# A decayed-state attention and a soft mixture of experts in one kernel: a pipeline of 24 chunk steps over eight heads, rewritten as 32 units of a head pair times three chunks

## The chip, the cores and the metric

The kernel runs on one core of a Trainium2 chip. The metric is the device time of one execution in microseconds (us); three executions of the kernel before took 251.03, 251.22 and 251.81 us, so its time is 251.22 us. A core has a matrix engine (TensorE, in the profile PE, its weight loads PEld), a vector engine (VectorE, DVE), a scalar engine (ScalarE, ACT) and GpSimd (POOL). SyncE (SP) here only issues transfers. Sixteen DMA engines carry the transfers of all queues. Matrix products are written to PSUM; the other data lie in SBUF.

## The reference

`r`, `k` and `v` are float32 arrays of shape 4 x 8 x 768 x 48 (batch, head, time, width), `w` and `u` are 8 x 48. The first half is a recurrence over time for every batch and head. Its output, with the heads laid side by side, is the 3072 x 384 input of the second half, a soft mixture of 8 experts with 4 slots each.

```python
# first half, for every batch b and head h
state = 0                                   # 48 x 48
for t in range(768):
    y[t]  = r[t] @ (state + outer(u * k[t], v[t]))
    state = w[:, None] * state + outer(k[t], v[t])

# second half: x is 3072 x 384, phi 384 x 32, w1 8 x 384 x 1024, w2 8 x 1024 x 384
logits = x @ phi
d = softmax over the 3072 rows of logits    # dispatch weights
slot_input = d.T @ x                        # 32 x 384: 8 experts x 4 slots
slot_out[e] = relu(slot_input[e] @ w1[e]) @ w2[e]
c = softmax over the 32 slots of logits     # combine weights
out = c @ slot_out                          # 3072 x 384
```

The maxima that the softmaxes subtract are left out here and in both kernels.

A chunked form of the recurrence lets the matrix engine do the work: inside a chunk of 128 time steps, with k and r scaled by powers of w, the part that stays in the chunk is a masked product of the scaled r and k with v, and the part from earlier chunks is the scaled r times a carried 48 x 48 state. The term with `u` is a number per time step and head, times v.

## The kernel before

A step is one chunk of one batch, with all eight heads: 4 x 6 = 24 steps. The transfers of a step are r, k and v of 128 x 8 x 48 floats; every row of 48 floats (192 bytes) lies by itself in the source. A weight of one expert is loaded by GpSimd's queue in some of the steps and turned from float32 to bfloat16 on the way.

```python
for b in range(B):
    state = st_pool.tile([D, H, D], bf, name="state")
    nc.vector.memset(state[:], 0.0)
    for c in range(nC):
        n_tile = b * nC + c
        issue_w_dma(n_tile - 8)                # w1[e] for 8 steps, then w2[e] for 8 steps
        r_ld, k_ld, v_ld = ...                 # in_pool, 3 buffers each
        nc.sync.dma_start(out=r_ld[:], in_=r[b, :, t0:t0 + C, :].rearrange("h p d -> p h d"))
        nc.sync.dma_start(out=k_ld[:], in_=k[b, :, t0:t0 + C, :].rearrange("h p d -> p h d"))
        nc.scalar.dma_start(out=v_ld[:], in_=v[b, :, t0:t0 + C, :].rearrange("h p d -> p h d"))
        nc.scalar.copy(v_bf[:], v_ld[:])
        nc.gpsimd.tensor_mul(rr2_cd[:], r_ld[:], W_neg3)      # scaled r
        nc.gpsimd.tensor_mul(kk_cd[:], k_ld[:], W_k3)         # scaled k
        nc.gpsimd.tensor_mul(ku[:], k_ld[:], u_rep3)
        nc.gpsimd.tensor_mul(ku[:], ku[:], r_ld[:])
        nc.vector.tensor_reduce(d_diag[:], ku[:], axis=mybir.AxisListType.X, op=ALU.add)
        for h in range(H):
            nc.tensor.transpose(rr2_dp[:, h, :], rr2_cd[:, h, :], ident[:])
            nc.tensor.transpose(kk_dp[:, h, :], kk_cd[:, h, :], ident[:])
        nc.scalar.copy(rr2_dc[:], rr2_dp[:])
        nc.scalar.copy(kk_dc[:], kk_dp[:])
        for h in range(H):
            nc.tensor.matmul(AT_p[:, h, :], kk_dc[:, h, :], rr2_dc[:, h, :])
        nc.vector.tensor_mul(AT_s[:], AT_p[:], mask_ut[:, None, :].to_broadcast([128, H, 128]))
        for h in range(H):
            nc.tensor.matmul(y_p[:, h, :], AT_s[:, h, :], v_bf[:, h, :], start=True, stop=False)
            nc.tensor.matmul(y_p[:, h, :], rr2_dc[:, h, :], state[:, h, :], start=False, stop=True)
        nc.gpsimd.tensor_mul(dv[:], v_bf[:], d_diag[:, :, None].to_broadcast([128, H, D]))
        nc.vector.tensor_add(x_sbuf[:, n_tile, :]..., y_p[:], dv[:])
        for h in range(H):
            nc.tensor.matmul(s_p[:, h, :], kk_cd[:, h, :], v_bf[:, h, :])
        nc.vector.tensor_add(state2[:], state[:], s_p[:])
        nc.gpsimd.tensor_mul(state[:], state2[:], w128_dc[:, :, None].to_broadcast([D, H, D]))
```

After all steps come three stages, one after the other: the routing (for each of 24 row tiles: three transposes of x, three products with phi, an exponential, the column sums, three products for the slot inputs, one transpose of the exponentials), the experts (`ht_p`, a rectifier for every 128 x 4 result, `so_p`), and the output:

```python
for ni in range(nN):                            # 24 tiles
    nc.tensor.matmul(o_p[:], LexpT[:, ni, :], so_sm[:, :])
    nc.vector.tensor_scalar_mul(o_s[:], o_p[:], rsum_r[:, ni:ni + 1])
    nc.sync.dma_start(out=out_ap[:, ni, :], in_=o_s[:])       # o_s has 3 buffers
```

Of the kernel before, what the change touches and what calls it, by code (L numbers as in the profile page):

```python
# [10 lines left out]
def kernel(  # L12
# [12 lines left out]
    nc = tc.nc  # L25
    B, H, S, D = r.shape
# [3 lines left out]
    assert Nn == B * S and Dm == H * D  # L30
# [3 lines left out]
    Spe = ES // E  # L34
    nN = Nn // C
    nM = Dm // C

    f32 = mybir.dt.float32
    bf = mybir.dt.bfloat16
    AF = mybir.ActivationFunctionType  # L40
    ALU = mybir.AluOpType

    cst = ctx.enter_context(tc.tile_pool(name="cst", bufs=1))

    ident = cst.tile([128, 128], bf)
    make_identity(nc, ident)

    mask_ut = cst.tile([128, 128], f32)
    make_upper_triangular(nc, mask_ut, val=1.0, diag=False)

    w_rep = cst.tile([128, H * D], f32, name="w_rep")
    nc.sync.dma_start(out=w_rep[:], in_=w.flatten().partition_broadcast(128))
    u_rep = cst.tile([128, H * D], f32, name="u_rep")
    nc.sync.dma_start(out=u_rep[:], in_=u.flatten().partition_broadcast(128))

    logw = cst.tile([128, H * D], f32, name="logw")
    nc.scalar.activation(out=logw[:], in_=w_rep[:], func=AF.Ln)

    iotash = cst.tile([128, 1], mybir.dt.int32, name="iotash")
    nc.gpsimd.iota(iotash, pattern=[[0, 1]], base=-C, channel_multiplier=1)  # L60
    ishf = cst.tile([128, 1], f32, name="ishf")
    nc.vector.tensor_copy(ishf[:], iotash[:])
    ishf2 = cst.tile([128, 1], f32, name="ishf2")
    nc.vector.tensor_scalar(out=ishf2[:], in0=ishf[:], scalar1=-1.0, scalar2=-1.0,
                            op0=ALU.mult, op1=ALU.add)

    W_neg = cst.tile([128, H * D], f32, name="W_neg")
    nc.scalar.activation(out=W_neg[:], in_=logw[:], func=AF.Exp, scale=ishf[:])  # L68
    W_k = cst.tile([128, H * D], f32, name="W_k")
    nc.scalar.activation(out=W_k[:], in_=logw[:], func=AF.Exp, scale=ishf2[:])  # L70

    w_hd = cst.tile([H, D], f32, name="w_hd")
    nc.sync.dma_start(out=w_hd[:], in_=w)
    ident_f32 = cst.tile([H, H], f32, name="ident_f32")
    make_identity(nc, ident_f32)
    w128_dc = cst.tile([D, H], f32, name="w128_dc")
    with tc.tile_pool(name="wT_ps", bufs=1, space=bass.MemoryType.PSUM) as wT_ps:
        wT_p = wT_ps.tile([D, H], f32, name="wT_p")
        nc.tensor.transpose(wT_p[:], w_hd[:], ident_f32[:])
        nc.scalar.activation(out=w128_dc[:], in_=wT_p[:], func=AF.Ln)  # L80
    nc.scalar.activation(out=w128_dc[:], in_=w128_dc[:], func=AF.Exp, scale=float(C))

    ones_col = cst.tile([128, 1], bf, name="ones_col")
    nc.vector.memset(ones_col[:], 1.0)

    x_pool = ctx.enter_context(tc.tile_pool(name="x_pool", bufs=1))
    x_sbuf = x_pool.tile([128, nN, Dm], bf, name="x_sbuf")
    nF = F // 128
    w1_all = x_pool.tile([128, E, nM, F], bf, name="w1_all")
    w2_all = x_pool.tile([128, E, nF, Dm], bf, name="w2_all")  # L90
    w1_ap = moe_w1.rearrange("e (mo p) f -> p e mo f", p=128)
    w2_ap = moe_w2.rearrange("e (fo p) d -> p e fo d", p=128)

    def issue_w_dma(idx):
        if 0 <= idx < E:
            nc.gpsimd.dma_start(out=w1_all[:, idx, :, :], in_=w1_ap[:, idx, :, :])
        elif E <= idx < 2 * E:
            ee = idx - E
            nc.gpsimd.dma_start(out=w2_all[:, ee, :, :], in_=w2_ap[:, ee, :, :])

    W_neg3 = W_neg[:].rearrange("p (h d) -> p h d", h=H)
    W_k3 = W_k[:].rearrange("p (h d) -> p h d", h=H)
    u_rep3 = u_rep[:].rearrange("p (h d) -> p h d", h=H)

    with tc.tile_pool(name="in_pool", bufs=3) as in_pool, \
         tc.tile_pool(name="st_pool", bufs=2) as st_pool, \
         tc.tile_pool(name="wk_pool", bufs=2) as wk_pool, \
         tc.tile_pool(name="ps_pool", bufs=1, space=bass.MemoryType.PSUM) as ps_pool, \
         tc.tile_pool(name="ps2_pool", bufs=1, space=bass.MemoryType.PSUM) as ps2_pool:

        for b in range(B):
            state = st_pool.tile([D, H, D], bf, name="state")
            nc.vector.memset(state[:], 0.0)

            for c in range(nC):
                n_tile = b * nC + c
                issue_w_dma(n_tile - 8)
                t0 = c * C
                r_ld = in_pool.tile([128, H, D], f32, name="r_ld")
                k_ld = in_pool.tile([128, H, D], f32, name="k_ld")  # L120
                v_ld = in_pool.tile([128, H, D], f32, name="v_ld")
                nc.sync.dma_start(out=r_ld[:], in_=r[b, :, t0:t0 + C, :].rearrange("h p d -> p h d"))
                nc.sync.dma_start(out=k_ld[:], in_=k[b, :, t0:t0 + C, :].rearrange("h p d -> p h d"))
                nc.scalar.dma_start(out=v_ld[:], in_=v[b, :, t0:t0 + C, :].rearrange("h p d -> p h d"))
                v_bf = in_pool.tile([128, H, D], bf, name="v_bf")
                nc.scalar.copy(v_bf[:], v_ld[:])  # L126

                rr2_cd = wk_pool.tile([128, H, D], bf, name="rr2_cd")
                kk_cd = wk_pool.tile([128, H, D], bf, name="kk_cd")
                nc.gpsimd.tensor_mul(rr2_cd[:], r_ld[:], W_neg3)  # L130
                nc.gpsimd.tensor_mul(kk_cd[:], k_ld[:], W_k3)  # L131

                ku = wk_pool.tile([128, H, D], f32, name="ku")
                nc.gpsimd.tensor_mul(ku[:], k_ld[:], u_rep3)  # L134
                nc.gpsimd.tensor_mul(ku[:], ku[:], r_ld[:])  # L135
                d_diag = wk_pool.tile([128, H], f32, name="d_diag")
                nc.vector.tensor_reduce(d_diag[:], ku[:], axis=mybir.AxisListType.X, op=ALU.add)  # L137

                rr2_dp = ps_pool.tile([D, H, C], bf, name="rr2_dp")
                kk_dp = ps_pool.tile([D, H, C], bf, name="kk_dp")  # L140
                for h in range(H):
                    nc.tensor.transpose(rr2_dp[:, h, :], rr2_cd[:, h, :], ident[:])  # L142
                    nc.tensor.transpose(kk_dp[:, h, :], kk_cd[:, h, :], ident[:])  # L143
                rr2_dc = wk_pool.tile([D, H, C], bf, name="rr2_dc")
                kk_dc = wk_pool.tile([D, H, C], bf, name="kk_dc")
                nc.scalar.copy(rr2_dc[:], rr2_dp[:])  # L146
                nc.scalar.copy(kk_dc[:], kk_dp[:])  # L147

                AT_p = ps2_pool.tile([128, H, 128], f32, name="AT_p")
                for h in range(H):  # L150
                    nc.tensor.matmul(AT_p[:, h, :], kk_dc[:, h, :], rr2_dc[:, h, :])  # L151
                AT_s = wk_pool.tile([128, H, 128], bf, name="AT_s")
                nc.vector.tensor_mul(  # L153
                    AT_s[:],
                    AT_p[:],
                    mask_ut[:, None, :].to_broadcast([128, H, 128]),
                )

                y_p = ps_pool.tile([128, H, D], f32, name="y_p")
                for h in range(H):  # L160
                    nc.tensor.matmul(y_p[:, h, :], AT_s[:, h, :], v_bf[:, h, :], start=True, stop=False)  # L161
                    nc.tensor.matmul(y_p[:, h, :], rr2_dc[:, h, :], state[:, h, :], start=False, stop=True)  # L162
                dv = wk_pool.tile([128, H, D], bf, name="dv")
                nc.gpsimd.tensor_mul(dv[:], v_bf[:], d_diag[:, :, None].to_broadcast([128, H, D]))  # L164
                nc.vector.tensor_add(  # L165
                    x_sbuf[:, n_tile, :].rearrange("p (h d) -> p h d", h=H),
                    y_p[:], dv[:])

                s_p = ps_pool.tile([D, H, D], f32, name="s_p")
                for h in range(H):  # L170
                    nc.tensor.matmul(s_p[:, h, :], kk_cd[:, h, :], v_bf[:, h, :])
                state2 = st_pool.tile([D, H, D], f32, name="state2")
                nc.vector.tensor_add(state2[:], state[:], s_p[:])
                nc.gpsimd.tensor_mul(state[:], state2[:], w128_dc[:, :, None].to_broadcast([D, H, D]))  # L174
# [14 lines left out]
    with tc.tile_pool(name="lg_ps", bufs=2, space=bass.MemoryType.PSUM) as lg_ps, \  # L189
# [5 lines left out]
        for ni in range(nN):  # L195
            xt_p = lg_ps.tile([128, nM, 128], bf, name="xt_p")
            for mi in range(nM):
                nc.tensor.transpose(xt_p[:, mi, :], x_sbuf[:, ni, mi * 128:(mi + 1) * 128], ident[:])  # L198
# [95 lines left out]
```

The softmax here doesn't subtract the row's maximum and nothing guards it: scores larger than these inputs give would overflow.

## Time and profile before

The profiled execution spans 249.5 us from its first to its last instruction. The chain that ended last and the busy time in windows divide it:

| stage | from, to (us) | what runs |
|---|---|---|
| start | 0 to 14 | first loads, tables of powers of w |
| 24 chunk steps | 14 to 177.7 | all engines |
| routing | 177.7 to 205.8 | PE 25.0 of 26 us in the middle part |
| experts | 205.8 to 224.3 | 384 matmuls, 64 rectifiers |
| slot outputs turned | 224.3 to 225.7 | 3 transposes |
| output | 225.7 to 249.5 | 24 products, 24 transfers |

Busy times over the span are PE 189.1 us, POOL 144.7, DVE 100.6, ACT 79.2. "Busy" for PE counts each matmul from its start to its end, though they run into each other, so starts of neighbouring matmuls say more than busy time. In a row of a group the last figures before the bar's end are busy us and the mean ns of one; in a window row the columns are PE, PEld, DVE, ACT and POOL busy with counts, the granted clock of the matrix engine, the busy share of the DMA engines and the GB/s that they wrote. That share can pass 1, as packets overlap.

### The profile page before, as it was taken

How to read it: one execution, taken by the hardware profiler on the slowest of the kernel's cores; microseconds unless marked ns; L12 is line 12 of the kernel's file. 1: busy time of each engine (PE TensorE's matmuls, PEld its weight loads, DVE VectorE, ACT ScalarE, POOL GpSimd, SP SyncE). 2: the span in 40 equal slices, each digit the busy share in tenths (PEclk: the TensorE clock that was granted, in tenths of full speed). 3: DMA queues.
4: the chain of work that ended last, by engine and by line, in shares of the span. 5: the costliest groups of instructions: out<-in, count | busy, mean ns of one | idle time of the engine just before them, and what ended most of it. 6: DMA issues, size and time to landing. Idle time of an engine off the chain costs nothing. (4 is left out here: it accounts for less than half of the span.)

```text
span 249.5 us, 4643 instructions
## 1 busy us (share of the span) xinstructions
PE 189.1 (76%) x1828; PEld 137.9 (55%) x1828; DVE 100.6 (40%) x209; ACT 79.2 (32%) x169; POOL 144.7 (58%) x171
## 2 busy tenths in 40 slices
PE   0049898899499999897696579675799978885552
PEld 0047686688277877675475357544566647771110
DVE  1012552653454554344232351434345551116673
ACT  2393433435135235323432133303011115540000
POOL 1389999999999997889578776982100000000000
PEclk9999999999555555555555555555555555555555
DMA  5998699696799999999999989490000000003655
GB/s 120 192 221 161 121 200 201 119 172 137 137 185 133 187 176 177 169 176 167 204 171 189 206 133 124 75 129 0 8 4 1 0 3 3 3 3 119 241 208 189
DMA packets 90581, 32.20 MB, mean 129 GB/s; under 512 B 75968, under 2 KB 87488, under 8 KB 90560
## 3 DMA queue, kind: packets, MB, share of 16 engines
q0 software_dynamic: 11520, 12.58, 32.8%
q1 hardware_dynamic: 54080, 14.60, 25.6%
q10 hardware_dynamic: 24960, 4.72, 10.0%
q8 instruction: 14, 0.23, 0.4%
q14 instruction: 7, 0.06, 0.1%
HBM read 39.77 MB, written 4.72 MB: 178 GB/s over the span
## 5 line engine op out<-in xcount | busy, mean ns | idle before, releaser
L146 ACT COPY rr_dc<-rr_dp 48x1024 bf16<-48x1024 bf16 x24 | 24.1, 1005 | 74.7 <-PE rr_dp L142 63.2
L142 PE MATMUL rr_dp<-ident,rr_cd 128*48 128x128 bf16 x192 | 32.2, 308 | 20.1 <-POOL rr_cd L130 16.1
L161 PE MATMUL y_p<-v_bf,AT_s 128*128 128x48 bf16 x192 | 42.5, 221 | 6.3 <-DVE AT_s L153 6.3
L162 PE MATMUL y_p<-state,rr_dc 48*128 48x48 bf16 x192 | 41.8, 217 | 0.4 <-POOL state L174 0.4
L142 PEld LDWEIGHTS <-rr_cd 128*48 128x48 bf16 x192 | 22.4, 153 | 22.4 <-POOL rr_cd L130 21.2
L153 DVE TENSOR_TENSOR AT_s<-AT_p,mask_ut 128x1024 bf16<-128x1024 f32 x24 | 29.3, 1221 | 12.6 <-PE AT_p L151 12.6
L165 DVE TENSOR_TENSOR x_sbuf<-y_p,dv 128x384 bf16<-128x384 f32 x24 | 13.4, 557 | 51.2 <-PE y_p L162 51.2
L174 POOL TENSOR_TENSOR state<-state,w_dc 48x384 bf16<-48x384 f32 x24 | 19.8, 825 | 22.8 <-PE y_p L162 22.5
L143 PE MATMUL kk_dp<-ident,kk_cd 128*48 128x128 bf16 x192 | 30.5, 308 | 1.2 <-POOL kk_cd L131 1.1
L161 PEld LDWEIGHTS <-AT_s 128*128 128x128 bf16 x192 | 20.0, 104 | 18.7 <-DVE AT_s L153 8.1
L137 DVE TENSOR_REDUCE d_diag<-ku 128x8 f32<-128x384 f32 x24 | 13.2, 548 | 38.7 <-POOL ku L135 38.7
L134 POOL TENSOR_TENSOR ku<-k_ld,u_rep 128x384 f32<-128x384 f32 x24 | 23.7, 987 | 8.1 <-DMA k_ld<-in_k_dram 8.1
L147 ACT COPY kk_dc<-kk_dp 48x1024 bf16<-48x1024 bf16 x24 | 24.1, 1004 | 7.1 <-PE kk_dp L143 7.1
L151 PE MATMUL AT_p<-rr_dc,kk_dc 48*128 48x128 bf16 x192 | 24.3, 303 | 1.6 <-ACT kk_dc L147 1.6
L143 PEld LDWEIGHTS <-kk_cd 128*48 128x48 bf16 x192 | 21.9, 151 | 5.1 <-POOL kk_cd L131 2.6
L162 PEld LDWEIGHTS <-rr_dc 48*128 48x128 bf16 x192 | 19.5, 101 | 9.5
L130 POOL TENSOR_TENSOR rr_cd<-r_ld,W_neg 128x384 bf16<-128x384 f32 x24 | 23.6, 985 | 1.3 <-ACT W_neg L68 1.3
L135 POOL TENSOR_TENSOR ku<-ku,r_ld 128x384 f32<-128x384 f32 x24 | 23.7, 986 | 0.1
L131 POOL TENSOR_TENSOR kk_cd<-k_ld,W_k 128x384 bf16<-128x384 f32 x24 | 23.7, 986 | 0.0
L151 PEld LDWEIGHTS <-kk_dc 48*128 48x128 bf16 x192 | 18.4, 136 | 3.3 <-ACT kk_dc L147 1.8
L164 POOL TENSOR_TENSOR dv<-v_bf,d_diag 128x384 bf16<-128x384 bf16 x24 | 19.7, 823 | 0.4 <-DVE d_diag L137 0.4
L126 ACT CAST v_bf<-v_ld 128x384 bf16<-128x384 f32 x24 | 12.3, 510 | 19.8 <-PE y_p L161 5.6
(63 smaller groups left out, 223.6 us busy)
## 6 DMA issues: line engine op xcount, KB each, us to landing
w_all<-in_moe_w_dram POOLq DMA_DIRECT2D x16, 768.0 KB, 7.8
v_ld<-in_v_dram ACTq DMA_DIRECT2D x24, 192.0 KB, 5.7
r_ld<-in_r_dram SPq DMA_DIRECT2D x24, 192.0 KB, 3.7
k_ld<-in_k_dram SPq DMA_DIRECT2D x24, 192.0 KB, 4.6
out_dram<-o_s SPq DMA_DIRECT2D x24, 192.0 KB, 1.9
w_rep<-in_w_dram SPq DMA_DIRECT2D x1, 192.0 KB, 3.9
u_rep<-in_u_dram SPq DMA_DIRECT2D x1, 192.0 KB, 6.2
phi_f<-in_moe_phi_dram SPq DMA_DIRECT2D x1, 48.0 KB, 1.9
```

The source lines that it names most:

```text
L130: nc.gpsimd.tensor_mul(rr2_cd[:], r_ld[:], W_neg3)
L131: nc.gpsimd.tensor_mul(kk_cd[:], k_ld[:], W_k3)
L134: nc.gpsimd.tensor_mul(ku[:], k_ld[:], u_rep3)
L135: nc.gpsimd.tensor_mul(ku[:], ku[:], r_ld[:])
L142: nc.tensor.transpose(rr2_dp[:, h, :], rr2_cd[:, h, :], ident[:])
L143: nc.tensor.transpose(kk_dp[:, h, :], kk_cd[:, h, :], ident[:])
L146: nc.scalar.copy(rr2_dc[:], rr2_dp[:])
L147: nc.scalar.copy(kk_dc[:], kk_dp[:])
L151: nc.tensor.matmul(AT_p[:, h, :], kk_dc[:, h, :], rr2_dc[:, h, :])
L153: nc.vector.tensor_mul(AT_s[:], AT_p[:], mask_ut[:, None, :].to_broadcast([128, H, 128]),)
L161: nc.tensor.matmul(y_p[:, h, :], AT_s[:, h, :], v_bf[:, h, :], start=True, stop=False)
L162: nc.tensor.matmul(y_p[:, h, :], rr2_dc[:, h, :], state[:, h, :], start=False, stop=True)
```

## The change

The whole kernel is rewritten. A unit is now one pair of heads over three chunks; there are 4 batches x 2 groups of three chunks x 4 pairs = 32 units. The powers of w count over the 384 steps of the three chunks (one frame), so no state has to be rescaled inside a unit: the state before each of its chunks is a prefix sum that PSUM accumulates. The pair's two 48-wide heads lie in a 128-wide tile at 0 and 64, so one transpose serves two heads. All instructions keep the program order on their engine, and each pass of the loop holds stages of up to four units; the routing of finished units lies in the passes too.

What it is for: fewer and larger operations on each engine, GpSimd with two multiplications per unit instead of six per chunk, no stage in which one engine alone works, and an output that is written in larger pieces.

The core of the diff (`O(...)` only records program order; the lines of the old loop, all removed, are those shown above):

```diff
+ def rows(src, b): return src[b].rearrange("h (c p) d -> p (h c) d", p=128)
+ def load_batch(b):                                   # two buffers for each of k, r, v
+     sp.dma_start(out=k_raw[b % 2][:], in_=rows(k, b))
+     sp.dma_start(out=r_raw[b % 2][:], in_=rows(r, b))
+     sp.dma_start(out=v_raw[b % 2][:], in_=rows(v, b))
+ load_batch(0); sp.dma_start(out=phi_f[:], ...); load_batch(1)
+ # w2 by "(p fo) d -> p fo d": eight rows of 384 in one piece for a partition; w1 as before
+ for c in range(L): W_k[:, c, :] and W_r[:, c, :] = Exp(scale * ln w)   # ACT, L = 3
+ def scale(i, j):   pool.tensor_mul(kr[:, j] (two heads at 0 and 64), raw k or r, W_k or W_r)
+ def v_cast(i):     act.copy(vb[:], raw_view(v_raw, i))
+ def t_pe(i):       6 x pe.transpose(Tb[i % 2][:, o:o + C], kr[:, j, c, :], ident[:])
+ def t_evac(i):     act.copy(krT, Tb[i % 2][:, 0:768])
+ def prod_f(i):     dve.tensor_mul(prod, Tb[i % 2][:, 0:384], krT[:, 1])     # k times r, for the u term
+ def a_pe(i):       6 x pe.matmul(Ab[:, e, c*C:(c+1)*C], krT[s, 0, c, :], krT[s, 1, c, :])  # s: 64 rows
+ def mask_f(i):     dve.tensor_mul(AT[:], Ab[:, :, 0:384], mask_ut broadcast)
+ def m_pe(i):       # group 0: 3 matmuls of 288, 192, 96 columns; group 1: ident, Z0 (192), then 192, 96
+     for c in range(nreg): pe.matmul(Mb[:, c*96:nreg*96], kr[:, 0, c, :], v of chunk c repeated, ...)
+     for c in range(L):    pe.matmul(Mb[:, 288+2*c:290+2*c], prod[:, c, :], ucol[:, q, :], ...)
+ def z_evac(i):     dve.tensor_mul(dv, v, Mb u terms); dve.tensor_mul(Z, Mb, bmask)
+                    if g == 0: dve.scalar_tensor_tensor(Z0, Mb, wT, bmask)
+ def y_pe(i):       6 x pe.matmul(48 columns: AT, vb); 2 or 3 x pe.matmul(96 columns: krT, Z)
+                    pe.matmul(Yb[:, 0:288], ident, dv)
+ def y_evac(i):     act.copy(x[:, :, pair], Yb)
+ def route_pe / route_act:   # for each three chunks (four units): 9 transposes of x, 9 products with phi,
+                    # 3 transposes and 12 products of the exponentials; ACT: 3 copies, 1 Exp, 1 copy
+ W_AT = {1: 1, 4: 1, 6: 1, 9: 1, 12: 1, 14: 1, 16: 1, 18: 1, 21: 1, 23: 2, 24: 2, 25: 3}
+ for i in range(-3, nH + nQ + 1):                     # nH = 32, nQ = 4
+     t_pe(i + 2); t_evac(i + 2)
+     scale(i + 3, 0); scale(i + 3, 1); v_cast(i + 3)
+     a_pe(i + 1); mask_f(i + 1)
+     prod_f(i + 2)
+     y_pe(i); y_evac(i)
+     m_pe(i + 1); z_evac(i + 1)
+     route_pe(i); route_act(i)
+     if i == 5: load_batch(2)
+     if i == 13: load_batch(3)
+     W_AT.get(i, 0) x load_w(...)                     # w1[0..7], then w2[0..7]
+ # experts: all 192 matmuls of w1 (columns fo:F:nF), one rectifier per expert on 128 x 32;
+ # then all 192 matmuls of w2, one copy per expert; 3 transposes and one copy
+ # output: row tiles i::24, six PSUM buffers, scaled by DVE and ACT in turn,
+ # transfers of 2, 4, 4, 4, 4, 4, 2 tiles; a partition's rows of one transfer are one piece
- for ni in range(nN): ... (routing, experts and output as stages of their own)
```

## The prediction

> **What bounds the kernel now.** I read the 40 slices first, then the DMA queues, the groups of instructions, the busy time in windows, and last the PE timeline, whose start-to-start times replace its busy time. Slices and queues:
>
> ```profile
> POOL 1389999999999997889578776982100000000000
> PEclk9999999999555555555555555555555555555555
> DMA  5998699696799999999999989490000000003655
> ...
> q0 software_dynamic: 11520, 12.58, 32.8%
> q1 hardware_dynamic: 54080, 14.60, 25.6%
> q10 hardware_dynamic: 24960, 4.72, 10.0%
> ```
>
> GpSimd fills the first 17 slices or so: it has four multiplications of 986 ns and two of about 824 ns per chunk, 5.6 us, and weight issues of about 0.9 us. The chunk steps take (177.7 - 14)/24 = 6.8 us each, so they are GpSimd's pace with some hand-over waits. The waits agree: DVE and ACT wait for PE and POOL, and a wait for a load is rare. But the second bound is near: the DMA row is at 9 from 6 to 143 us. The rest of the span, 71.8 us, is the three late stages (28.1 routing, 19.9 experts with the turned slot outputs, 23.8 output), in which the DMA row is empty or half full and GpSimd idle.
>
> How fast can the loads go? Windows (GB/s is the last column, DMA share before it):
>
> ```profile
> 12.00:14.00 2.00, 0.00 (x0) 0.00 (x0) 0.00 (x0) 1.97 (x4) 0.84 (x1) 1.00 1.32 247
> 15.00:18.00 3.00, 2.19 (x24) 2.06 (x23) 1.10 (x2) 2.97 (x6) 3.00 (x5) 1.00 1.15 213
> 22.00:23.50 1.50, 1.50 (x13) 1.06 (x11) 0.37 (x1) 0.36 (x1) 1.50 (x3) 1.00 1.10 218
> 155.00:158.00 3.00, 1.33 (x14) 1.02 (x14) 2.19 (x4) 0.45 (x1) 2.89 (x4) 0.50 1.30 202
> ```
>
> The first and third are full of 192-byte rows alone (the third from one queue), 218 to 247 GB/s; I take 230. The second is a w1 load, the fourth a w2 load, 202 to 213 GB/s at their bfloat16 destination. So a batch of k, r and v (3.54 MB) needs 15.4 us and a weight (0.786 MB) 3.75 us: all of it 4 x 15.4 + 16 x 3.75 = 122 us of full DMA. In the packets of the trace between 16.5 and 17.5 us, 103 weight packets of 2 KB pass and about 20 of 192 bytes: a weight in flight nearly stops the input rows.
>
> PE, from the timeline (start, length, x count):
>
> ```profile
> 48.99 0.51 PE L171 MATMUL s_p<-v_bf,kk_cd 128*48 128x48 bf16 x8
> ...
> 49.65 1.03 PE L151 MATMUL AT_p<-rr_dc,kk_dc 48*128 48x128 bf16 x8
> ...
> 52.12 0.22 PE L161 MATMUL y_p<-v_bf,AT_s 128*128 128x48 bf16 x1
> 52.27 0.22 PE L162 MATMUL y_p<-state,rr_dc 48*128 48x48 bf16 x1
> 52.42 0.22 PE L161 MATMUL y_p<-v_bf,AT_s 128*128 128x48 bf16 x1
> ```
> ```profile
> 60.66 0.60 PE L151 MATMUL AT_p<-rr_dc,kk_dc 48*128 48x128 bf16 x8
> ```
>
> Eight products of 128 columns in 1.03 us, less the 0.30 us of the last one, over seven: about 105 ns apart, 1.2 columns per ns. The same eight take 0.60 us at 60.66, in the only stretch of fast clock (58.4 to 61.8 us). So the nines of the PEclk row before 58 us are not a fast clock; PE ran at half speed nearly throughout. 48-column products follow 42 ns apart (s_p), but 153 ns apart in y_p, where a 128-row and a 48-row product alternate: about 110 ns for each change of form.
>
> **What the Trainium skill says.** "DMA: Bandwidth & Descriptors", Specifications, asks for at least 512 bytes per transfer for line rate. The trace agrees in direction: 192-byte rows move at 218 to 247 GB/s, the 1536-byte output rows at up to 241 though they come in separate transfers with gaps. The changed kernel keeps the 192-byte rows. Its section "Queues, rings and completion order" says that an engine takes turns between queues by packets, not bytes; that is what starves the 192-byte rows beside 2 KB packets here. "TensorE: Matmul & The Clock Gate", Part 1, gives 107 ns (cold) and 56 ns (warm) for 128 columns; the trace has 105 and, in its one warm stretch, about 60. "TensorEngine Tiling (Array Packing)", Key Properties, says that a change of tiling mode drains the engine; the 153 against 42 ns agree.
>
> **The change, part by part. PE per unit.** Columns: transposes 768; `a_pe` 768; `m_pe` 576 or 480, mean 528, and 6; `y_pe` 6 x 48 + 240 + 288 = 816 (240 is the mean of two and three of 96). Routing per three chunks 9 x 128 + 9 x 32 + 3 x 128 + 12 x 32 = 2208, for a unit 552. Sum 3438 columns, at 1.2 per ns 2.87 us. Two changes of form around the 64-row `a_pe` add 0.2, the tiny products 0.1; if the two 64-row halves overlap, some 0.3 comes off. I take 3.0 us.
>
> **The others per unit.** ACT: 384 elements take 510 ns and 1024 take 1005 (rows L126 and L146), so 213 + 0.773 n: 0.81 (768) + 2 x 0.44 (288) + routing (3 x 0.51 + 0.29 + 0.51)/4 = 0.58, sum 2.3 us. DVE: 384 take 557, 1024 take 1221 (L165, L153), so 158 + 1.04 n: mask 0.96, product 0.36 to 0.56, dv 0.46, Z 0.36, half a Z0 0.13, sum 2.3 to 2.5. GpSimd: two multiplications of 288 at about 0.78, and half a weight issue of 0.9, sum 2.0; eight heads of one chunk are 4/3 units, so 2.7 us against 5.6 plus issues before. No instruction waits for one later than the pass before or the head of its own, so a pass lasts as long as its busiest engine: PE, 3.0 us. Without waits for loads the 32 units take 96 us.
>
> **Loads against units.** First packets came 1.9 us after their issue at 0.75. From 2.65: w_rep 0.7, then k, r, v of batch 0 at 5.1 each: v has landed at about 19.5 with its completion. `v_cast(0)` holds ACT till then; three short filling passes, unit 0 at 22.5. Batch 1 and phi and the weights of passes 1 and 4 end at 2.65 + 0.7 + 30.8 + 0.3 + 7.5 = 42; pass 5 (which casts unit 8) would come at 22.5 + 5 x 3 = 37.5 and waits till 42.5. Batch 2 follows with three weights, 15.4 + 11.2, to 69; pass 13 by the engines at 66.5, so 69. Batch 3 with the weights of passes 14, 16, 18: 69 + 26.6 = 96, or with pass 21's too, 99; by the engines 93; I take 97. The other 11 units: 97 + 33 = 130. The seven weights of passes 23 to 25 need 26 us from about 103 on and are in by then. Five passes of routing alone at 1.2 us: 136. Of this some 12 us are waits for loads.
>
> **Tail.** Experts: in the old stage w1 or w2 matmuls without a rectifier between come about 30 ns apart (eight in 0.35 to 0.37 us, the last 0.17). 384 x 0.031 = 12, and 2 us for reciprocals, the first multiplication, three transposes and copies: 14, against 19.9. The old output sends one transfer of 192 KB at a time, 1.9 us to landing, and waits for the buffer. The new one scales on two engines (24 x 0.62/2 = 7.4 us) so the transfer binds: 4.72 MB at about 400 GB/s (1536 bytes in 60 ns on each of 16 engines, from the trace's packets) 11.8, first tiles and issue 2, end 1: 15, against 23.8.
>
> 136 + 14 + 15 = 165 us span; time before exceeds span by 1.7: **167 us**. Of the 84 saved, 70 are chunk steps and routing (205.8 - 136), of which the routing stage alone is 28; 6 are experts and 9 output, with rounding.
>
> **Rivals.** (1) *Loads bind outright.* If the mixed stream keeps only about 165 GB/s on the 192-byte rows, as 6 us windows of the old kernel show where issue stalls, a batch takes 21 us and the main part ends near 158: 190 us. For it: DMA at 9 for 130 us before, and the same rows. Against: those windows had small transfers held by buffers; here six large ones queue. (2) *PE turns fast.* Columns now stream without gaps, which before held for only one stretch of 3.4 us. Then PE needs 1.8 us, DVE with hand-overs 2.6 to 2.8 binds, and the loads more so: main part near 128, 155 to 160 us. Against: with PE waiting again the clock may fall back. (3) *Hand-overs bind.* If banks shared by several uses (Xb, Tb) tie engines together within a pass, a pass lasts 4 us: 22.5 + 128 + 6 + 29 = 187 us. For it: the old kernel's 6.8 us against GpSimd's 6.2 to 6.5. Against: each stage reads results of the pass before. (4) *The strided weight loads* (columns fo:F:nF) may not come at 30 ns; at 60 the tail grows by 6 us.
>
> **Range and chances.** Rivals 1 and 3 reach 187 to 190, rival 2 down to 155; a low end with both fast clock and loads at 247 GB/s is 150. I give 150 to 188. To be within 2% or slower, 80 us would have to be lost on top; only a mistake in the whole reading does that: faster 0.96, same 0.01, slower 0.03.
>
> **What would show it.** Right: first y_p after 20 to 25 us; ACT's v_cast or POOL's scale waiting for v_raw or k_raw near passes 5, 13 and 21, some 12 us in all; passes of 3.0 us between; routing ended near 136; experts 14; output 15 with DMA near full. Wrong: passes over 3.6 us with no load wait (rival 3), waits for loads over 25 us (rival 1), PEclk at 9 or 1.0 and DVE without idle time (rival 2), weight loads of w1 over 45 ns apart (rival 4). The prediction fails as a whole if a pass is set by something I have not summed.

## The result, and the profile after

The changed kernel takes 165.32 us (four executions, 164.9 to 166.12) against 251.44 us for the kernel before: a ratio of 0.658 (95% interval 0.656 to 0.660). The prediction was 167.0 us. The profiled execution spans 163.1 us. The slices and the queues of the changed kernel, in the places of those shown of the kernel before:

```profile
POOL 2011737992004889999201516996000000000000
PEclk9999999996555799999995555999995555555555
DMA  3999999999998999999999794899999600002996
...
q1 hardware_dynamic: 20032, 18.92, 45.7%
q0 software_dynamic: 4352, 12.58, 39.4%
```

Three things are to be seen. The DMA row is at 8 or 9 from the second slice to the end of the weights at 130 us, but for a 7 and a 4 between 90 and 102 us: loads and weights now form one nearly full stream. (The 4 lies where batch 3 has ended, at 96.5 us, and the next weights are not issued before 100.9.) GpSimd is no longer full; it has two long holes, and so have PE and ACT. And the PEclk row has nines in most of the main part, this time real ones. The trace grants the full clock from 27.4 to 37.6, from 54.7 to 85.4 and from 102.5 to 123.0 us, and half of it from 37.6 to 54.7 and from 85.4 to 102.5, that is in most of each hole and for 5 to 7 us after it. The timeline of PE in that part (start, length, x count) has

```profile
71.47 0.50 PE L188 MATMUL Tb<-ident,kr 128*128 128x128 bf16 x6
71.90 0.34 PE L206 MATMUL Ab<-krT 64*128 64x128 bf16 x6
72.17 0.32 PE L261 MATMUL Yb<-v_bf,AT 128*128 128x48 bf16 x6
```

The next group starts 0.43 us after the first of six transposes, 72 ns for each 128 columns, where the kernel before needed about 105.

The holes are the waits of ScalarE for v. The timeline of ACT around them (the idle time before an instruction stands in brackets, with what ended it):

```profile
33.98 0.80 ACT L193 COPY krT<-Tb 128x768 bf16<-128x768 bf16 x1
47.68 0.43 ACT L181 CAST v_bf<-v_raw 128x288 bf16<-128x288 f32 x1 [12.89 <-DMA v_raw<-in_v_dram]
...
80.50 0.79 ACT L193 COPY krT<-Tb 128x768 bf16<-128x768 bf16 x1
97.23 0.43 ACT L181 CAST v_bf<-v_raw 128x288 bf16<-128x288 f32 x1 [15.95 <-DMA v_raw<-in_v_dram]
```

These are the casts of the first units of batch 1 (pass 5) and of batch 3 (pass 21). Between the holes a pass takes 2.04 us on average (copies of y at 48.0 and 78.6 us, 15 passes apart), and 1.85 us in the part at the full clock (65.7 and 78.6 us, seven apart). Most passes there take 1.7 us; every fourth, which holds the routing's products of the exponentials, takes 2.7 to 2.9. Busy time in windows, from the start to the first y, over the first stretch, the first hole, and then the middle, the second hole, the last units, the last routing, the experts and the output:

```profile
0.00:23.80 23.80, 4.40 (x37) 2.63 (x37) 4.93 (x20) 8.14 (x16) 6.61 (x17) 1.00 0.88 196
23.80:34.00 10.20, 9.27 (x142) 7.21 (x139) 10.10 (x26) 7.56 (x17) 8.96 (x12) 1.00 1.03 217
34.00:50.00 16.00, 3.52 (x62) 3.00 (x58) 3.55 (x9) 3.11 (x8) 3.43 (x6) 0.61 1.11 235
...
62.00:82.00 20.00, 18.46 (x354) 14.85 (x351) 19.13 (x46) 16.96 (x40) 16.13 (x22) 1.00 1.12 229
82.00:100.00 18.00, 3.43 (x39) 2.69 (x40) 2.19 (x6) 2.59 (x7) 4.25 (x6) 0.59 0.98 212
...
117.40:124.40 7.00, 3.60 (x61) 2.34 (x59) 0.45 (x3) 3.51 (x9) 0.00 (x0) 0.90 1.04 216
124.40:146.50 22.10, 19.54 (x412) 19.27 (x413) 2.64 (x12) 1.61 (x9) 0.00 (x0) 0.50 0.22 45
146.50:163.10 16.60, 8.44 (x24) 3.62 (x23) 7.36 (x12) 6.98 (x12) 0.00 (x0) 0.50 0.70 284
```

In the middle stretch PE, VectorE and ScalarE are all nearly full; in the holes none is, while the last two figures of the row (DMA share, GB/s) stay at 0.98 to 1.11 and at 212 to 235. The 86 us saved divide into 81.4 for chunk steps and routing (205.8 to 124.4), 7.2 for the output (23.8 to 16.6), and a loss of 2.2 for the experts (19.9 to 22.1), a stage in which PE still works nearly alone (19.5 of 22.1 us).

### The profile page after: what moved, and what is told of

Read it like the earlier page. It is cut to its first block, busy times and chain, and to the rows that moved or that the text cites. A ratio compares the mean times of both kernels' runs of the same rounds, so it can differ in the third digit from the quotient of the medians.

```text
span 163.1 us, 3869 instructions
## 1 busy us (share of the span) xinstructions
PE 98.1 (60%) x1580; PEld 77.1 (47%) x1580; DVE 75.7 (46%) x184; ACT 73.9 (45%) x166; POOL 61.0 (37%) x89
## 3 DMA queue, kind: packets, MB, share of 16 engines
HBM read 39.57 MB, written 4.72 MB: 272 GB/s over the span
## 4 chain that ended last, share of the span: by engine, by line
PE 28%; SPq 25%; DMA 24%; ACT 8%; POOL 4%; DVE 4%; issue 3%; ACTq 0%; DVEq 0%
DMA v_raw<-in_v_dram 24%; SPq L96 17%; PE Ab L393 4%; SPq L97 4%; SPq L100 3%; POOL kr L175 3%; PE Tb L393 2%; PE Mb L393 2%; PE Ab L402 2%; PE Tb L188 2%; PE Ab L421 2%; SPq L95 1%; ACT r_raw L425 1%; ACT xT L298 1%; ACT krT L193 1%
## 5 line engine op out<-in xcount | busy, mean ns | idle before, releaser
L175 POOL TENSOR_TENSOR kr<-k_raw,W_k 128x288 bf16<-128x288 f32 x32 | 25.6, 801 | 41.4 <-PE Mb L235 25.2
L211 DVE TENSOR_TENSOR AT<-Ab,mask_ut 128x768 bf16<-128x768 f32 x32 | 30.5, 952 | 16.0 <-PE Ab L206 15.7
L181 ACT CAST v_bf<-v_raw 128x288 bf16<-128x288 f32 x32 | 13.9, 433 | 38.0 <-DMA v_raw<-in_v_dram 38.0
L188 PE MATMUL Tb<-ident,kr 128*128 128x128 bf16 x192 | 20.0, 243 | 17.6 <-POOL kr L175 17.3
L175 POOL TENSOR_TENSOR kr<-r_raw,W_r 128x288 bf16<-128x288 f32 x32 | 25.6, 799 | 9.7 <-DMA r_raw<-in_r_dram 9.7
L193 ACT COPY krT<-Tb 128x768 bf16<-128x768 bf16 x32 | 25.4, 795 | 4.6 <-PE Tb L188 3.8
L188 PEld LDWEIGHTS <-kr 128*128 128x128 bf16 x192 | 13.4, 108 | 19.9 <-POOL kr L175 19.8
L244 DVE TENSOR_TENSOR dv<-v_bf,Mb 128x288 bf16<-128x288 bf16 x32 | 14.3, 446 | 0.3
L280 ACT CAST x<-Yb 128x288 bf16<-128x288 f32 x32 | 12.6, 395 | 2.3 <-PE Yb L273 1.5
L232 PE MATMUL Mb<-v_bf,kr 128*128 128x192 bf16 (+2 forms) x80 | 12.9, 267 | 0.0
L232 PEld LDWEIGHTS <-kr 128*128 128x128 bf16 x80 | 8.5, 110 | 2.4 <-issue 0.2
## 6 DMA issues: line engine op xcount, KB each, us to landing
w_all<-in_moe_w_dram POOLq DMA_DIRECT2D x16, 768.0 KB, 11.6
```

Of the source, the lines that this page charges most:

```text
L175: O(pool.tensor_mul(kr[:, j].rearrange("p c (h s) -> p c h s", s=64)[:, :, :, 0:D], raw_view((k_raw, r_raw)[j], i), W_kr[j][:, :, 2 * q:2 ...
L181: O(act.copy(vb[:], raw_view(v_raw, i)))
L188: O(pe.transpose(Tb[i % 2][:, o:o + C], kr[:, j, c, :], ident[:]))
L193: O(act.copy(krT[:].rearrange("p j c t -> p (j c t)"), Tb[i % 2][:, 0:2 * T]))
L211: O(dve.tensor_mul(AT[:], Ab[:, :, 0:T].rearrange("p e (c t) -> p e c t", c=L), mask_ut[:, None, None, :].to_broadcast([128, 2, L, C])))
L232: O(pe.matmul(o, kr[:, 0, c, :], vc, start=first, stop=True, skip_group_check=True))
```

## The experiments

My theory after the result: the end of the main part is set by the stream of loads and weights, and the experts lost what the strided columns of w1 cost. The rival: the engines' pace sets the main part, and the waits for v only hide it.

**The engines alone.** Batches 2 and 3 and fourteen of the sixteen weights are not loaded; their units and experts compute on what is there. The arithmetic of all engines stays; fourteen weight issues on GpSimd go too.

```diff
-        if i == 5: load_batch(2)
-        if i == 13: load_batch(3)
-    W_AT = {1: 1, 4: 1, 6: 1, ...}
+    W_AT = {1: 1, 4: 1}                # w1[0], w2[0] alone, read by all experts
```

> The changed kernel that leaves out the loads of batches 2 and 3 (their units compute on the data of batches 0 and 1) and fourteen of sixteen weights (all experts use expert 0's); every instruction of the five engines stays. Loads bind: one wait at pass 5 till about 40 us, then 27 passes of 1.9 us and the routing, main part ends near 98, span about 137. Engines bind: main part ends near 124 as in the changed kernel, span 160 or more.

Measured, in one execution: 143.39 us, span 141.6; routing ends at 102.7, some 5 us later than forecast. Windows of this run, up to the end of the wait at pass 5, to the end of the routing, and experts:

```profile
0.00:45.00 45.00, 15.03 (x210) 10.79 (x211) 18.33 (x50) 16.66 (x33) 17.91 (x31) 0.93 0.91 198
45.00:103.00 58.00, 51.46 (x935) 41.21 (x935) 47.13 (x111) 47.65 (x114) 34.04 (x44) 0.91 0.01 3
103.00:124.80 21.80, 19.55 (x411) 19.14 (x411) 2.35 (x12) 1.58 (x8) 0.00 (x0) 0.50 0.01 2
```

In the second row the DMA share is 0.01 and nothing waits for a load: 26 passes take 50.9 us, 1.96 each. The same arithmetic ends 21.7 us earlier, so the loads bind the main part. That rival falls. The missing issues on GpSimd do not explain it: passes 14 to 20, where the changed kernel waits for no load either, take 12.9 us in both.

**Weights late.** Same bytes, other order.

```diff
-    W_AT = {1: 1, 4: 1, 6: 1, 9: 1, 12: 1, 14: 1, 16: 1, 18: 1, 21: 1, 23: 2, 24: 2, 25: 3}
+    W_AT = {19: 1, 20: 1, 21: 2, 22: 2, 23: 2, 24: 2, 25: 2, 26: 2, 27: 2}
```

> The changed kernel with all sixteen weights issued in passes 19 to 27 instead of 1 to 25; the bytes are the same. Loads set the end of the main part (my theory): without weights in between, v of batch 1 lands at about 36 us instead of 47.6 and v of batch 3 at about 68 instead of 97, so the waits of ACT for v_raw fall from 38 to under 15 us and routing ends near 95 instead of 124; then the experts wait for the last weights, which end near 128 as before; span about 147, time about 149. Engines set the pace of the main part (rival): waits for loads only hide engine time, routing ends at 124 plus or minus 2 and the time stays at 165.

Measured: 158.97 us, ratio to the kernel before 0.633 (0.630 to 0.636), against 165.32 of the changed kernel. The waits for v fell to 17.3 us, v of batch 3 ended at 74 instead of 97 us, but the main part still ended near 118. Waits of this run (total us, times, longest):

```profile
ACT v_bf L181 <- DMA v_raw<-in_v_dram: 17.3, 4, 9.9
...
POOL w_all L108 <- DMA w_all<-in_moe_w_dram: 14.2, 6, 3.1
```

The second line was not foreseen. From the eleventh weight on GpSimd's issue waited until an earlier weight had landed, eight being under way, and the scaling of later units stood behind it in program order: passes of 7.5 us at units 27 to 29. The load theory gave the right direction; the gain went into a new wait.

**Weights late, without that wait.**

```diff
+    W_AT = {19: 1, 20: 1, 21: 1, 22: 1, 23: 1, 24: 1, 25: 1, 26: 1, 28: 2, 29: 2, 30: 2, 31: 2}
```

> The changed kernel with weights in passes 19 to 26 (eight) and 28 to 31 (eight), so that GpSimd never holds back a unit's scaling while it waits for an earlier weight to land. If that wait made the first late version slow (its passes of 7.5 us at units 27 to 29): routing ends near 105 instead of 118, the experts wait for the last weight, which lands at 133 as before, span 151 to 153, time 153 to 155. If it did not matter: time 158 to 160 as in the first late version.

Measured: 153.02 us, ratio 0.608 (0.607 to 0.610), the fastest of all versions here; span 152.0. Its windows for the loads, the last units and routing, the experts and the output:

```profile
0.00:74.00 74.00, 47.94 (x782) 37.63 (x783) 49.22 (x122) 46.04 (x101) 43.03 (x64) 0.95 0.92 201
74.00:101.80 27.80, 21.76 (x388) 17.13 (x388) 16.86 (x41) 18.77 (x46) 17.39 (x25) 0.91 1.12 212
101.80:135.40 33.60, 18.47 (x388) 17.72 (x388) 2.02 (x10) 1.58 (x8) 0.53 (x1) 0.50 0.94 193
135.40:152.00 16.60, 8.44 (x24) 3.63 (x23) 7.36 (x12) 6.96 (x12) 0.00 (x0) 0.50 0.70 284
```

The main part now ends at 99.4 us (the third row begins where the experts' first product does), and the experts wait for the last weight, which lands at 133. The wait of GpSimd was the cause of the lost gain. What is left is the stream itself (from 2.5 to 133 us) and what must follow it.

**Columns of w1 next to each other.**

```diff
-    w1_all[:, e, mi, fo:F:nF]                               w2: "(p fo) d -> p fo d"
+    w1_all[:, e, mi, fo * C:(fo + 1) * C]                   w2: "(fo p) d -> p fo d"
```

> The changed kernel with the columns of w1 for one matmul next to each other (and w2 loaded in rows of 768 bytes to fit). Strided weight loads theory: the w1 matmuls come 27 to 30 ns apart instead of 60, 192 x 0.032 = 6 us less, experts 16 instead of 22 us, time 159. Rival (half clock or the waits for the rectifier make them slow): less than 1.5 us change, time 164 to 166.

Measured: 164.58 us, 0.655 (0.653 to 0.658): nearly no gain. Yet the experts changed as the theory said. Weight loads of the experts, first in the changed kernel (w1, then w2), then in this one:

```profile
L393 PEld LDWEIGHTS <-w_all 128*128 128x128 bf16 x192 | 11.8, 170 | 0.6 <-issue 0.6
L402 PEld LDWEIGHTS <-w_all 128*128 128x128 bf16 x192 | 5.4, 104 | 0.7 <-issue 0.7
```
```profile
L393 PEld LDWEIGHTS <-w_all 128*128 128x128 bf16 x192 | 5.4, 104 | 0.7 <-issue 0.7
L402 PEld LDWEIGHTS <-w_all 128*128 128x128 bf16 x192 | 5.3, 104 | 0.7 <-issue 0.7
```

Start to start, the w1 matmuls went from 60 to 27 ns, and their stage from 12.4 to 6.0 us. But it began at 132.95 instead of 126.79 us. The trace divides these 6.2 us. ScalarE's cast of batch 3's v came 2.8 us later, in a run in which one weight started earlier (see the output runs below). The ten passes after it took 23.8 instead of 20.8 us (one of them, with three weights before it, 4.2); the issue of a w2 load takes GpSimd 911 ns instead of 571, for the eight of them 2.7 us, which is about as much, though no run shows it by itself. So the strided columns cost 6 us where they stand, and in this version the main part ended 6 us later.

**An earlier start.**

```diff
+    if b == 0:                      # in load_batch
+        for q in range(nQ):         # k, r, v of one head pair after another
+            for t, src in ((k_raw, k), (r_raw, r), (v_raw, v)):
+                sp.dma_start(out=t[j][:, s, :], in_=rows(src, b)[:, s, :])
```

> The changed kernel with the loads of batch 0 in four parts, k, r and v of one head pair at a time, so that unit 0 can start near 10 us instead of 22. Loads bind: the early start is lost again in a longer wait at pass 5, since the stream of transfers is as long as before; v of batch 3 lands at 97 plus or minus 3, time 163 to 166. Engines bind (each pass counts): 10 us less, time 155.

Measured: 166.03 us in the fastest of four executions; the other three, with the profiled one among them, are 2.2 to 2.9% slower, and a loss that only these show is not put down to the edit. In the profile the first y was copied at 20.4 instead of 24.8 us, not near 10: that copy stands behind the cast of unit 3, the last pair, on ScalarE. Passes 5, 13 and 21 copied theirs at 43.7, 72.9 and 102.6 us, and v of batch 3 ended at 101.8 us, 5 us later than in the changed kernel; nine weights instead of eight had landed before it. The early start was lost, as the load theory says: even the fastest execution is not below the changed kernel's 165.32.

**The three edits together** (late weights of the first form, w1 columns, early start):

> The changed kernel with three edits together: weights in passes 19 to 27, w1 columns next to each other, batch 0 in four parts. If the stream of transfers now is the only bound, the last weight lands at 127 to 131 us whatever starts earlier, and the output follows at once: span 147 to 150, time 149 to 152, no better than the late weights alone. If the edits add up (16 + 6 + 10 us), time 133 to 138.

Measured: 155.77 us, 0.619 (0.615 to 0.622). The last weight ended at 134.1 us and the output began at 137.3. The gains do not add: the stream ends at 133 to 134 us in all three late versions. It is 3.2 us faster than the late version on which it builds and 2.75 us slower than the second one. The last eight weights, w2 in rows of 768 bytes, landed 3.85 us apart, in large pieces 3.7; in the profiles, which are 1.8 us apart, 0.9 us is the later landing of the last weight, and the output began 3.0 instead of 2.0 us after that landing.

**What sets the pace of a pass without loads.** Two runs on top of the one with few loads. In the first, VectorE's dv is left out (a zero tile stands in for it, so the u term is missing):

```diff
-        dve.tensor_mul(dv, v, Mb u terms)
+        st["dv", i] = dvz
```

> The changed kernel with few loads (batches 2 and 3 and fourteen weights left out), which also leaves out VectorE's dv multiplication: a zero tile is added in its place, so the u term is missing. In the run with few loads 26 passes took 50.9 us, 1.96 each. If VectorE sets that pace (its starts there add up to about 2.0 us per unit), the pass falls by up to the 0.37 us of dv to 1.6 to 1.75, where ScalarE comes next, and the span to about 135 us. If PE sets it, the pass stays at 1.9 to 2.0 and the span at 141.

In the second, every transpose of k and r and every k-r product is issued twice:

```diff
+                for _ in range(2):
                     pe.transpose(...)     # and likewise pe.matmul(Ab[...])
```

> The changed kernel with few loads, and each transpose of a unit and each k-r product issued twice: twelve matmuls more per unit, about 0.5 us of PE at the fast clock. If PE sets the pace of 1.96 us per pass: 2.4 us or more, span 153 or more. If VectorE sets it and PE has slack: under 2.15 us, span under 147.

Measured, one execution each: 140.65 us (span 138.9), 1.84 us per pass, and 149.78 us (span 148.0), 2.22 us per pass, against 1.96. Neither theory holds alone. Taking 0.37 us from VectorE gave 0.12, adding some 0.5 us to PE cost 0.26. Busy time in a stretch without waits for loads, with few loads, without dv, and with the doubled products:

```profile
48.00:80.00 32.00, 30.74 (x584) 24.99 (x584) 30.61 (x72) 28.73 (x69) 24.61 (x33) 0.98 0.01 3
46.00:76.00 30.00, 29.49 (x552) 24.69 (x550) 24.22 (x53) 27.19 (x65) 23.24 (x30) 0.91 0.01 4
50.00:82.00 32.00, 32.00 (x684) 28.07 (x682) 27.90 (x65) 26.68 (x62) 21.75 (x28) 1.00 0.01 3
```

Four passes in a row tell more than the mean. With few loads they take 2.88 us (the one with the routing's products of the exponentials), 1.69, 1.69 and 1.45 or 1.83. Without dv they take 2.46, 1.68, 1.68 and 1.44: the long pass and the last got shorter, the two in between did not, and in these ScalarE's four copies follow each other without idle time. With the doubled products they take 2.80, 2.07, 2.15 and about 1.98: the short ones grew, the long one did not. So by the traces ScalarE sets two of four passes, VectorE has a part in the other two, and PE with some 0.5 us more sets the short ones. No single engine sets 1.96; the busy shares of PE, VectorE and ScalarE, 0.90 to 0.96 in the first row, do not tell this.

**The bound of the kernel before.** GpSimd's two multiplications for the u term are left out there (the row sum reads r, so the output lacks the right u term).

```diff
-                nc.gpsimd.tensor_mul(ku[:], k_ld[:], u_rep3)
-                nc.gpsimd.tensor_mul(ku[:], ku[:], r_ld[:])
-                nc.vector.tensor_reduce(d_diag[:], ku[:], ...)
+                nc.vector.tensor_reduce(d_diag[:], r_ld[:], ...)
```

> The kernel before, leaving out GpSimd's two multiplications for the u term (the row sum reads r instead, so the output lacks the right u term). GpSimd bound it (my reading): 24 x 2 x 0.986 = 47 us of GpSimd time goes, and the next bound takes over, the loads (122 us of full DMA) or PE (4224 columns at 1.2 per ns and 16 changes of form, 5.3 us per chunk, 127 us), so the chunk steps take 130 instead of 164 us and the time is about 217. Loads bound it already: the chunk steps stay above 155 us, time above 241. Hand-overs between engines bound it: between the two, 225 to 240.

Measured: 240.19 us, ratio 0.956 (0.952 to 0.960). 47 us of GpSimd's work gave 11 us. The chunk steps of this run, and its waits:

```profile
14.00:165.00 151.00, 136.72 (x1152) 105.14 (x1153) 65.27 (x96) 60.05 (x74) 94.42 (x108) 1.00 0.96 165
...
ACT v_bf L126 <- DMA v_ld<-in_v_dram: 39.0, 11, 5.5
...
DVE d_diag L134 <- DMA r_ld<-in_r_dram: 15.2, 4, 7.5
```

In the kernel before ACT's cast waited 3.7 us for v. So GpSimd did bind it, but by some 11 us only; my forecast of 217 us was wrong, and the result lies at the upper edge of the third forecast, just under the sign of the second. Behind GpSimd stand the loads (39 and 15 us of waits in the two lines) and PE, busy for 137 of the 151 us; no run parts these two. My 122 us of full DMA was too little for that kernel: in this run its chunk steps took 151 us and moved 165 GB/s at a DMA share of 0.96.

**The output.** First the kernel before with only its output changed, four tiles to a transfer:

```diff
-            o_s = out_pool.tile([128, Dm], f32, name="o_s")          # one tile, one transfer
+            o_s = out_pool.tile([128, 4, Dm], f32, name="o_s")       # four tiles, DVE and ACT in turn
+            nc.sync.dma_start(out=out_ap[:, n0:n0 + 4, :], in_=o_s[:])
```

> The kernel before with only its output stage changed: four row tiles per transfer, scaled by DVE and ACT in turn, four PSUM buffers; rows of 1536 bytes as before. If the wait for a buffer after each small transfer made the old stage slow: 23.8 us fall to 16 or 17, time 244. If the size of a contiguous piece counts (1536 against 6144 bytes): under 3 us gained, time 248 to 251.

Measured: 245.01 us, ratio 0.976 (0.974 to 0.978): 6 us gained with the same rows of 1536 bytes. The stage fell from 23.8 to 17.8 us. The edit does three things at once (larger transfers, a second engine, more PSUM buffers). The group of VectorE's scalings in the kernel before shows what was to be had from the buffers: 5.7 us of waiting until an earlier transfer had landed, beside 14.2 us of work.

```profile
L262 DVE TENSOR_SCALAR o_s<-o_p,rsum_r 128x384 f32<-128x384 f32 x24 | 14.2, 616 | 6.6 <-DMA out_dram<-o_s 5.7 <-PE o_p L260 0.6
```

Then the changed kernel with single transfers, no buffer used twice:

```diff
-    sizes = [2, 4, 4, 4, 4, 4, 2]
+    sizes = [1] * 24
```

> The changed kernel with 24 transfers of one tile instead of seven; two engines scale and no buffer is used twice, as in the changed kernel. If the old output lost its time to waiting for a buffer: 0 to 1.5 us more, time 165 to 167. If small transfers or small pieces are slow in themselves: 5 to 7 us more, time 170 to 172.

Measured: 168.07 us, 0.669 (0.667 to 0.671), 2.7 us more than the changed kernel. But its output stage took 17.0 us, only 0.4 more. The rest lies ahead of the edit: pass 13 took 6.5 us instead of 2.9, because v of batch 2 ended at 67.7 instead of 62.8 us. So the size of a transfer is not what made the old output slow: small transfers without a buffer used twice cost 0.4 us. The wait for its buffers, 5.7 us, is about as large as the 6 us gained; what the second engine gave by itself was not tried.

Why did a load end 5 us later in a part that was not edited? I took it that the weight of pass 12 had slipped ahead of v's last rows, and moved it to pass 13:

```diff
-    W_AT = {..., 12: 1, ...}
+    W_AT = {..., 13: 1, ...}
```

> The kernel with 24 single output transfers, and the weight of pass 12 issued in pass 13. If its 2.7 us over the changed kernel came from that weight slipping ahead of the last rows of batch 2's v (issued at 62.2, v landed at 67.7; in the changed kernel 62.7 and 62.8), the wait in pass 13 falls by about 4 us and the time to 164 to 166. If the single transfers cost it: 167 to 169 as before.

Measured: 167.6 us, 0.667 (0.664 to 0.669); pass 13 still took 6.9 us. That reading falls. The packets of the traces show which weight it was: the one of pass 9, issued at 56.6 us in the changed kernel and at 56.1 here. Its first packet came 5.1 us after the issue in the changed kernel, behind most of v, and 1.5 to 2.0 us after it in the two runs with single transfers and in the run with w1's columns together. What decides this start is open, and no run moves that weight.

## Why the prediction was right, by its own steps

The total came out about 1% off (167.0 against 165.3) because two wrong terms cancelled, which is luck: the main part was 11.6 us too long, experts and output 9.7 us too short. Of the rivals, 2 and 4 both came true; rival 2's 155 to 160 us and rival 4's 6 us make 161 to 166. Step by step:

**The start** (v of batch 0 at 19.5, unit 0 at 22.5): v ended at 19.9 and was cast at 20.5, the first y matmul ran at 23.8. Right, about 1 us late.

**3.0 us per pass: wrong.** It was 1.85 us at the full clock, and 2.04 between the holes as a whole. The step that failed is "PE per unit ... at 1.2 per ns": it took the half clock of the kernel before for granted, with rival 2 as the exception. Rival 2's sign came true, PEclk at 9 in the main part, and the pass is then not PE's alone; "a pass lasts as long as its busiest engine" fits the passes of 1.69 us (ScalarE), not every fourth, of 2.7 to 2.9. What let the clock rise was not tried. At half clock, right after the first hole, two passes took 2.46 and 2.47 us, so the figure was high by 0.5 even there; the six 64-row products, 0.43 us instead of 0.64, are part of that, and neither pass holds the routing's products of the exponentials. VectorE's 2.3 to 2.5 was too high as well, by 0.3 to 0.5: its instructions start closer together (mask to product 0.87 us) than their durations.

**12 us of waits for loads: wrong in size, right in place.** The two long ones were 12.9 and 16.0 us, in passes 5 and 21; in pass 13 ScalarE did not wait. With 28.8 us in all the recorded sign of rival 1 (over 25 us) appeared too, though the last arrival came as forecast: the sign could not tell slow loads from fast units. The last arrival was well worked out: v of batch 3 cast at 97.2 against 97. It is a sum of transfers, four batches and the eight weights ahead of its end, and as long as these are the same, faster passes only wait longer. The two before it were off by 5 and 6 us in opposite directions: one weight more than I had counted ran beside the last rows of batch 1 (47.6 against 42.5 us; GpSimd, which does not wait for v, issued it at 36.7), and fewer had gone before the end of batch 2 (63.4 against 69). The rate of 230 GB/s for rows alone was too high: in the second late version, without weights in between, batches 1 to 3 took 17 to 18 us each, at 203 to 212 GB/s, not 15.4; in the changed kernel, with rows and weights side by side, the stream moved 229 GB/s between 62 and 82 us, and the sum came right.

**End of the main part 136, measured 124.4.** After v of batch 3 there are eleven units and the last routing: at 3.0 us per unit 39 us, at 1.9 us 27. That is the whole error of 12 us. The run with few loads and the late weights show that the loads and their order, not the sum of engine work, set this end.

**Experts 14, measured 22.1.** This is rival 4, which I had named and left out of the sum. The term of 0.031 us per matmul holds for w2 (27 ns), not for w1's strided columns (60 ns), 192 x 0.033 = 6.3 us; the other 1.75 us are the 24 row sums of the exponentials ahead of the experts, which I had not counted. "TensorE: Matmul & The Clock Gate", section "Weight-path perf modes", has the fast weight load work on packed or strided columns, for steps up to 1,024 elements; the measurement adds that the strided load is slower here, 170 against 104 ns.

**Output 15, measured 16.6**: 4.72 MB at up to 417 GB/s, with 2.3 us before the first packet. The packets of 1536 bytes that I read as 60 ns took 65 (median); the new ones of 6144 bytes took 235. The reason given, that the old stage waited for its buffers, is borne out by the 5.7 us in its trace and the two output runs.

**What bounded the kernel before**: GpSimd, with loads and PE 11 us behind; shown by the run without the u multiplications. My line that the DMA row is at 9 from 6 to 143 us misread it: up to 69 us four of its slices stand at 6 or 7. "No instruction waits for one later than the pass before" is consistent with passes as short as 1.7 us; rival 3 did not occur.

## What to carry to other kernels

When a transfer stream is full, place its arrivals on the time axis first, then hang the engine work on them: a faster pipeline then gives only what follows the last arrival, and a prefetch that is issued earlier can push a needed load back. Put bulk weights behind the loads that units wait for, and never let an engine that units need wait on the weights' queue: the two together were worth 12 us over the changed kernel, the first alone 6. A prediction whose total fits should be checked term by term: here 12 us too much in the main part and 10 too little after it cancelled.

## What the runs showed of the hardware that I had not expected

- The four batches, each loaded whole, appear as 18,432 packets of 768 bytes, four rows each, at 49 ns (median), where single-step loads and the loads by head pair appear as packets of 192 bytes at 15 ns. Beside a weight, packets alternate about one for one (80 and 79 per us between 72 and 76 us), so these rows got 61 GB/s; rows in 192-byte packets had got about 4 (20 packets per us beside 103 of the weight, so there the turns were not one for one, and taking turns by packets does not by itself explain how far those rows were held back). The stream as a whole moved 212 to 235 GB/s in the windows where its DMA share was near 1 or above.
- Strided stationary operands load more slowly: 170 ns against 104 for a step of 8 elements, and 157 against 101 for the step of 24 in the output's products.
- An issue of a weight on GpSimd's queue waited when eight earlier ones had not landed; whether the chip or the program's own semaphores ask for this is not shown. Large pieces take less of GpSimd: 571 against 911 ns per issue.
- VectorE's and ScalarE's instructions overlap at their ends: ScalarE's 0.80 us copies were followed after 0.69 us.
